# First expert layer of a pooled-attention chain: its last 768 tokens computed as one pair with seven half-depth products

## The chip, the core and the metric

The kernel runs on one core of a Trainium2 chip. The metric is the device time of one execution in microseconds (us); of several runs the median is given. TensorE does the matrix products, VectorE (DVE) and ScalarE (ACT) do the elementwise work and empty the accumulators, GpSimd (POOL) helps them, and SyncE (SP) issues most transfers. Each engine runs its instructions in the order of the program; they meet through semaphores.

## What is computed

Attention over keys and values averaged in groups of 8 (4 batches, 8 heads, 576 positions, 64 channels), then two expert layers over the 2304 tokens of 512 channels:

```python
def _moe_ref(x, w_gate, w_val, w_out):            # 512 -> 1536 -> 512
    gate = 1.0 / (1.0 + np.exp(-(x @ w_gate)))
    val = x @ w_val
    return (gate * val @ w_out).astype(np.float32)

def _moe2_ref(x, w_in, w_out):                    # 512 -> 2048 -> 512
    h = x @ w_in
    sp = np.where(h > 20.0, h, np.log1p(np.exp(np.minimum(h, 20.0))))
    g = h * np.tanh(sp)
    return (g @ w_out).astype(np.float32)
```

All inputs come as 64-bit numbers and are made 32-bit in the kernel; products are made from a high and a low part of each operand (three matmuls: high by high, high by low, low by high).

## The kernel before

**Tiles.** Tokens stand in 18 tiles of 128. The first layer goes through five blocks of 512, 384, 384, 512 and 512 tokens (`sizes`, L67). In a block the 12 slices f of 128 hidden channels follow one another. For each f, `part` (L545) makes the gate `pg` and then the value `pv`, each by 12 matmuls as wide as the block (4 slices of depth, 3 matmuls each); ScalarE makes the sigmoid (L860), VectorE the product (L866), ScalarE its high part (L869) and VectorE its low part (L873, in block 0 a word `G` at L711); `emit_out` (L727) then adds the slice f-1 into four accumulators with 12 more matmuls (`mm3`, L101). `finish` (L733) copies the accumulators out and stores them to `x2d` in DRAM.

**Between the matmuls.** After each of the three groups of 12 matmuls there is a slot (L818). In block 0 the slots run words of a hand-made plan, `START` (L20); the part of it ahead of the first bar runs before block 0. A word is a letter with its numbers and, after a colon, an engine: `m`, `M`, `X`, `N`, `t`, `c`, `p`, `h`, `l` are the attention steps of a tile (scores, maximum, exponent, norm, transpose, copy, values, high and low part of x); `C`, `A`, `B` turn a raw 64-bit weight into its 32-bit parts (scale, bits, high and low part); `K`, `Z`, `V` pool keys and values; `L`, `U`, `J`, `Q`, `R` load. In blocks 1 to 3 the attention of the next block is spread evenly over the slots (`att_tasks`, `batch_tasks`). The second layer's 32 weight pieces are converted in blocks 2 to 4 (`w2_step`): 16 input pieces are stored to `w2d`, 16 output pieces stay in SBUF, in the buffers of first-layer weights that are no longer read. In block 4 the slots prepare the second layer's first operands (`prep_x2`, `prep_w`).

**Second layer.** Three pairs of 2 x 384 tokens. The tokens of a pair and two slices of the weights form a 2 x 2 product that is made by seven half-depth products of sums (`product`, L971, six matmuls of 384 columns each), and `out_unit` (L941) multiplies by the output weights, 512 wide (L933).

**Memory that matters here.** Accumulators: 8 banks, four named `acc0` to `acc3`, two `mm`, two `at`. Output weights of the first layer are stored to `wod` once and read again for each block into a ring of three tiles named `wo` (`load_wo`, L556).

## Time and profile before

| | us |
|---|---|
| median of 3 runs (896.75 to 898.51) | 897.32 |
| span of the profiled execution | 895.9 |
| TensorE busy in it | 885.8 |
| VectorE busy | 520.7 |
| ScalarE busy | 428.3 |
| GpSimd busy | 81.3 |

The span runs from the first to the last instruction of one profiled execution; the median of the timed runs lies 1.4 us above it, for what lies around the instructions. Matmuls overlap: a row that says 0.33 us for one matmul does not say that the next one starts 0.33 us later, and the distance between two starts is what a matmul costs in a row of many.

### The profile page before, as it was taken

The numbers are of one execution on the slowest core, as the hardware profiler recorded it, in microseconds if no ns is written. First come the engines' busy times: TensorE is split into PE (matmuls) and PEld (weight loads), VectorE is DVE, ScalarE is ACT, GpSimd is POOL, SyncE is SP. The second block draws the span as 40 slices with busy tenths as digits, with TensorE's granted clock in tenths as the row PEclk, the third lists the DMA queues.
The fourth block names the chain that finished last, engine by engine and source line by source line (L and its number), as shares of the span: only waits on it lengthen the run. The fifth ranks groups of instructions, "written<-read, shape, count | busy, mean of one in ns | idle before, by whom it ended". The sixth has DMA issues, their size and how long they took to land.

```text
span 895.9 us, 12736 instructions
## 1 busy us (share of the span) xinstructions
PE 885.8 (99%) x4780; PEld 790.3 (88%) x4780; DVE 520.7 (58%) x990; ACT 428.3 (48%) x991; POOL 81.3 (9%) x90
## 2 busy tenths in 40 slices
PE   8999999999999999999999999999999999999998
PEld 7877889999999988888888899998899998999986
DVE  6779864332453332332577467776677767677632
ACT  7756664243454554343445244445454445444431
POOL 3566430100020000000000000000000000000000
PEclk9999999999999999999999999999999999999999
DMA  7788654433575544334665231211121202110001
GB/s 270 227 293 269 223 188 152 135 126 101 166 249 183 172 153 153 118 105 154 211 223 189 71 118 48 83 47 61 35 83 48 83 24 94 59 48 24 1 36 36
DMA packets 42362, 113.33 MB, mean 127 GB/s; under 512 B 5820, under 2 KB 10684, under 8 KB 42300
## 3 DMA queue, kind: packets, MB, share of 16 engines
q1 hardware_dynamic: 41004, 110.25, 37.0%
q10 hardware_dynamic: 1296, 2.26, 0.7%
q8 instruction: 38, 0.62, 0.3%
q14 instruction: 24, 0.20, 0.1%
HBM read 92.42 MB, written 20.07 MB: 126 GB/s over the span
## 4 chain that ended last, share of the span: by engine, by line
PE 90%; DMA 4%; ACT 3%; DVE 2%; issue 1%; SPq 0%; POOL 0%; ACTq 0%; DVEq 0%
PE acc L933 22%; PE p L104 7%; PE p L102 7%; PE p L103 7%; PE acc L102 5%; PE acc L104 5%; PE acc L103 5%; PE pv L550 5%; PE pv L551 5%; PE pv L554 5%; PE pg L550 5%; PE pg L551 5%; PE pg L554 5%; DMA raw<-wv 2%; PE pv L462 2%; PE sc L406 2%
## 5 line engine op out<-in xcount | busy, mean ns | idle before, releaser
L933 PE MATMUL acc<-w,g 128*128 128x512 f32 x864 | 201.3, 390 | 0.0
L933 PEld LDWEIGHTS acc<-w,g 128*128 128x128 f32 x864 | 161.7, 188 | 33.0 <-DVE g L927 0.3
L866 DVE TENSOR_TENSOR sg<-sg,pv 128x512 f32<-128x512 f32 (+1 forms) x58 | 36.5, 629 | 139.5 <-PE pv L554 127.1
L102 PE MATMUL acc<-gh,wo 128*128 128x512 f32 (+1 forms) x240 | 90.2, 376 | 0.0
L103 PE MATMUL acc<-gl,wo 128*128 128x512 f32 (+1 forms) x240 | 88.6, 369 | 0.7 <-DVE gl L711 0.7
L104 PE MATMUL acc<-gh,wo 128*128 128x512 f32 (+1 forms) x240 | 88.4, 368 | 0.0
L550 PE MATMUL pg<-xh,wg 128*128 128x512 f32 (+1 forms) x232 | 86.5, 373 | 0.0
L550 PE MATMUL pv<-xh,wv 128*128 128x512 f32 (+1 forms) x232 | 85.7, 369 | 0.5 <-DVE sg L866 0.5
L551 PE MATMUL pg<-xl,wg 128*128 128x512 f32 (+1 forms) x232 | 85.2, 367 | 0.0
L551 PE MATMUL pv<-xl,wv 128*128 128x512 f32 (+1 forms) x232 | 85.0, 367 | 0.0
L860 ACT ACTIVATE sg<-pg 128x512 f32<-128x512 f32 (+1 forms) x58 | 32.1, 554 | 105.1 <-PE pg L554 104.9
L869 ACT CAST gh<-sg 128x512 fp32r<-128x512 f32 (+1 forms) x60 | 34.9, 582 | 93.7 <-DVE sg L866 93.7
L102 PE MATMUL p<-top,w2s 128*128 128x384 f32 x216 | 72.5, 335 | 0.0
L104 PE MATMUL p<-top,w2s 128*128 128x384 f32 x216 | 72.4, 335 | 0.0
L103 PE MATMUL p<-top,w2s 128*128 128x384 f32 x216 | 72.2, 334 | 0.0
L236 DVE SCALAR_TENSOR_TENSOR cv<-raw,cv 128x512 uint32<-128x512 uint32 x68 | 56.2, 826 | 2.3
L554 PE MATMUL pv<-xh,wv 128*128 128x512 f32 (+1 forms) x232 | 56.9, 366 | 0.0
L554 PE MATMUL pg<-xh,wg 128*128 128x512 f32 (+1 forms) x232 | 56.9, 366 | 0.0
L222 ACT ACTIVATE cv<-raw 128x512 f32<-128x512 f32 x66 | 44.9, 680 | 24.1 <-DMA raw<-wo 10.4
L873 DVE TENSOR_TENSOR gl<-sg,gh 128x384 fp32r<-128x384 f32 (+1 forms) x48 | 30.0, 625 | 36.4 <-ACT gh L869 36.4
L103 PEld LDWEIGHTS acc<-gl,wo 128*128 128x128 f32 x240 | 45.1, 188 | 6.7 <-DVE gl L711 1.0
L102 PEld LDWEIGHTS acc<-gh,wo 128*128 128x128 f32 x240 | 45.1, 188 | 6.7 <-issue 1.3
(150 smaller groups left out, 1674.8 us busy)
## 6 DMA issues: line engine op xcount, KB each, us to landing
wo<-wod SPq DMA_DIRECT2D x48, 512.0 KB
ws<-w2d SPq DMA_DIRECT2D x24, 512.0 KB
raw<-w2i SPq DMA_DIRECT2D x16, 512.0 KB
raw<-w2o SPq DMA_DIRECT2D x16, 512.0 KB
raw<-wv SPq DMA_DIRECT2D x12, 512.0 KB
raw<-wo SPq DMA_DIRECT2D x12, 512.0 KB
wod<-wo SPq DMA_DIRECT2D x12, 512.0 KB
raw<-wg SPq DMA_DIRECT2D x11, 512.0 KB
```

The lines of the kernel that those rows point to most:

```text
L102: nc.tensor.matmul(ps, wt[:, 0, cols], xh, start=start, stop=False)
L103: nc.tensor.matmul(ps, wt[:, 0, cols], xl, start=False, stop=False)
L104: nc.tensor.matmul(ps, wt[:, 1, cols], xh, start=False, stop=stop)
L222: eng.activation(out=f32(c), in_=hi, func=AF.Prelu, scale=BIAS, alpha=-(2.0**32))
L236: nc.vector.scalar_tensor_tensor(out=c, in0=lo, scalar=29, in1=c, op0=ALU.logical_shift_right, op1=ALU.bitwise_or)
L550: nc.tensor.matmul(ps[:, c0:c1], w, xh[:, k, c0:c1], start=(k == 0), stop=False)
L551: nc.tensor.matmul(ps[:, c0:c1], w, xl[:, k, c0:c1], start=False, stop=False)
L554: nc.tensor.matmul(ps[:, c0:c1], w, xh[:, k, c0:c1], start=False, stop=(k == KD - 1))
L860: nc.scalar.activation(out=sg, in_=pg[:, :n], func=AF.Sigmoid)
L866: nc.vector.tensor_mul(out=sg, in0=sg, in1=pv[:, :n])
L869: nc.scalar.copy(out=gh, in_=sg)
L933: nc.tensor.matmul(acc[t][0], g[:, a, c], w[:, b, :], start=(f == 0 and first), stop=(f == NF2 - 1 and last),)
```

## The change

The first layer now goes through three blocks of 512 tokens and then takes the last 768 tokens as one pair of 2 x 384. The pair uses the scheme of the second layer with gate and value in the place of two weight slices: for each f seven products of six matmuls, 384 wide, give gate and value of both halves of the tokens. The sums of weights that this needs (`split_sums`, words `S` and `D`) are made in blocks 1 and 2, stored to `wsd` in DRAM (`z`) and read back in the pair (`load_sums`, `prep_sums`). The sums of tokens are made by words `x` in the last seven slots of block 2, and by `late_rows` after them. The output product of the first half follows one f behind; the gated values of the second half (`g1`) stay in SBUF, and their output product, 12 x 12 matmuls, comes after the last f. GpSimd multiplies gate and value of the second half.

All slots of blocks 0 to 2 now follow the plan, which is new from the start on: attention of tiles 4 to 7 in block 0, 8 to 11 in block 1, 12 to 17 in block 2. Tile 7 is finished inside block 1: for its first f the gate and value are made for 384 tokens, then the words `t7` to `l7` run, then the last 128 tokens follow. All 32 weight pieces of the second layer are converted in blocks 1 and 2 (`d` load, `r` scale, `s` bits, `b` store); the output pieces go to a new DRAM tensor `w2od` and are read back and split in the pair (`split_w2o`). Seventeen of the stores `b` and `z` are issued by ScalarE's queue (`b:a`, `z:a`). In the new part ahead of the first bar and in block 0, eleven conversions have their low part on VectorE (`B:d`; three before) and eight on GpSimd behind ScalarE (`B:a`; nineteen before). The second layer's first operands are prepared during the 12 output steps at the end (`todo`). Work and code of the second layer stay, but its banks start with the accumulators `acc0` to `acc3`.

```diff
--- before.py
+++ after.py
...
+    NG = 384
+    sizes = [NB, NB, NB, 2 * NG]
...
+    w2od = [dram.tile([128, 512], F32, name=f"w2od{i}") for i in range(NF2)]
+    wsd = [dram.tile([128, 2, 512], F32, name=f"wsd{i}") for i in range(NF)]
...
+                if j == NBLK - 1:
+                    c, t0 = divmod(t0, NG)
+                    nc.scalar.copy(out=xs_t[0][:, :, c, t0 : t0 + 128], in_=ps.rearrange("p (k t) -> p k t", k=KD))
+                    return lambda: None
...
+            def split_sums(f):
+
+                t = wpool.tile([128, 2, 512], F32, tag="wo", name="ss", bufs=NWO)
+                G = nc.vector
+                a, b = slice(0, 256), slice(256, 512)
+                for i, nm in enumerate("gv"):
+                    w = w_in_t[nm, f]
+                    settle(w)
+                    G.tensor_add(out=t[:, i, :], in0=f32(w[:, 0, :]), in1=f32(w[:, 1, :]))
+
+                def rest():
+                    G.tensor_sub(out=t[:, 1, a], in0=t[:, 0, a], in1=t[:, 1, a])
+                    G.tensor_sub(out=t[:, 1, b], in0=t[:, 1, b], in1=t[:, 1, a])
+                    G.tensor_add(out=t[:, 0, a], in0=t[:, 0, a], in1=t[:, 1, b])
+                    G.tensor_sub(out=t[:, 0, b], in0=t[:, 0, b], in1=t[:, 1, b])
+
+                rest_of[f] = rest
+                store_of[f] = lambda eng: eng.dma_start(out=wsd[f], in_=t)
...
-                    soon.append(lambda m=m, x=x: nc.sync.dma_start(out=x2d[m][:, o : o + n], in_=x))
+                    later.append(lambda m=m, x=x: nc.sync.dma_start(out=x2d[m][:, o : o + n], in_=x))
...
+                steps = [hi(1, b11), lo(1, b11), sub(b11, b12, b11), hi(5, b11), sub(b12, b22, b12), hi(7, b12), lo(5, b11)]
+                steps += [sub(b11, b22, b11), hi(6, b11), lo(7, b12), lo(6, b11), sub(b12, b21, b11), hi(2, b21), lo(2, b21)]
+                return steps, [hi(4, b12), hi(3, b22), lo(4, b12), lo(3, b22)]
...
+            def load_sums(f):
+                t = sums_of[f] = pa.tile([128, 2, 512], F32, tag="raw", name="sl", bufs=3)
+                nc.sync.dma_start(out=t, in_=wsd[f])
...
+            def prep_sums(f):
+
+                t = sums_of.pop(f)
+                if f % 2:
+                    st = [x1c[:, 1024 * i : 1024 * i + 1024].rearrange("p (a n) -> p a n", a=2) for i in range(2)]
                 else:
+                    st = [px.tile([128, 2, 512], F32R, tag="s", name="s", bufs=2) for _ in range(2)]
+                sum_sets[f] = st
+                for i in (1, 0):
+                    nc.scalar.copy(out=st[i][:, 0, :], in_=t[:, i, :])
+                    nc.vector.tensor_sub(out=st[i][:, 1, :], in0=t[:, i, :], in1=f32(st[i][:, 0, :]))
...
+                    for word in plan[3 * NF * j + k + (1 if j == 0 else 2)]:
+                        run(word)
...
+                    if (j, f) == (1, 0):
+                        c0 = n - 128
+                        pv = ps_mm.tile([128, 512], F32, tag="mm", name="pv")
+                        part(pg, w_in_t["g", f], x_t[1], 0, c0)
+                        part(pv, w_in_t["v", f], x_t[1], 0, c0)
+                        for word in plan[3 * NF + 1]:
+                            run(word)
...
+            late_rows = pr["rows"][1][0][12:] + pr["rows"][0][1] + pr["rows"][1][1]
+            for fn in late_rows:
+                fn()
...
+            banks1 = [(ps_mm, "mm"), (ps_mm, "mm"), (ps_at, "at"), (ps_at, "at")]
+            o3 = blocks[-1][0]
+            wo_c = {}
+            V, A = nc.vector, nc.scalar
+            for f in range(NF):
+                gt, vt = w_in_t["g", f], w_in_t["v", f]
+                sA, sB = sum_sets[f][1], sum_sets[f][0]
+                where = {1: (gt, 0), 2: (gt, 256), 3: (sB, 256), 4: (vt, 256), 5: (sB, 0), 6: (sA, 256), 7: (sA, 0)}
+                a = pg_pool.tile([128, NG], F32, tag="sg", name="a", bufs=2)
+                u, v = (pg_pool.tile([128, NG], F32, tag="gh", name=t, bufs=2) for t in "uv")
+                y = pg_pool.tile([128, NG], F32, tag="gl", name="y", bufs=2)
+
+                def product(k):
+
+                    pool, tag = banks1[k % 4]
+                    ps = pool.tile([128, 512], F32, tag=tag, name=f"q{k}")
+                    wt, c0 = where[k]
+                    for kk in range(2):
+                        xh, xl = pr[k, kk]
+                        mm3(ps[:, :NG], wt, slice(c0 + 128 * kk, c0 + 128 * kk + 128), xh, xl, kk == 0, kk == 1)
+                    return ps[:, :NG]
+
+                wo_c[f] = load_wo(f)
+                p1 = product(1)
+                A.copy(out=a, in_=p1)
+                p6 = product(6)
+                V.tensor_add(out=u, in0=a, in1=p6)
+                p5 = product(5)
+                V.tensor_add(out=v, in0=u, in1=p5)
+                p7 = product(7)
+                V.tensor_add(out=y, in0=v, in1=p7)
+                V.tensor_add(out=u, in0=u, in1=p7)
+                if f + 1 < NF:
+                    prep_sums(f + 1)
+                if f + 2 < NF:
+                    load_sums(f + 2)
+                if f == 0:
+                    emit_out(prev[0], prev[1], prev[2], prev[3], acc_of[prev[0]], prev[4])
+                    finish(prev[0], acc_of.pop(prev[0]), prev[4])
+                    flush()
+                    flush()
+                else:
+                    if f == 1:
+                        acc = acc_tiles()
+                    out_384(wo_c.pop(f - 1), pend, acc, f == 1, False)
+                if f == NF - 1:
+                    wo_c2 = {i: load_wo(i) for i in range(2)}
+                    split_g1(0)
+                    split_g1(1)
+                p2 = product(2)
+                V.tensor_add(out=a, in0=a, in1=p2)
+                A.activation(out=a, in_=a, func=AF.Sigmoid)
+                p4 = product(4)
+                V.tensor_add(out=u, in0=u, in1=p4)
+                V.tensor_mul(out=a, in0=a, in1=u)
+                g = x1c[:, 2048 + 768 * (f % 2) : 2816 + 768 * (f % 2)].rearrange("p (a n) -> p a n", a=2)
+                A.copy(out=g[:, 0, :], in_=a)
+                p3 = product(3)
+                V.tensor_add(out=g1[f], in0=v, in1=p3)
+                A.activation(out=g1[f], in_=g1[f], func=AF.Sigmoid)
+                V.tensor_sub(out=g[:, 1, :], in0=a, in1=f32(g[:, 0, :]))
+                pend = g
+                nc.gpsimd.tensor_mul(out=g1[f], in0=g1[f], in1=y)
+                if f >= 3:
+                    for i in range(2):
+                        if 2 * (f - 3) + i < NF2:
+                            load_w2o(2 * (f - 3) + i)
+                if f >= 4:
+                    for i in range(2):
+                        split_w2o(2 * (f - 4) + i)
+                if f == NF - 1:
+                    load_x2(0, 0)
...
+            for f in range(2):
+                out_384(wo_c2.pop(f), gs.pop(f), acc2, f == 0, False)
+                split_g1(f + 2)
+                wo_c2[f + 2] = load_wo(f + 2)
+            out_384(wo_c.pop(NF - 1), pend, acc, False, True)
+            evict_384(acc, o3)
+            rows0 = prep_x2(0)
+            for _ in range(2):
+                w_sets.append(
+                    [wpool.tile([128, 2, 512], F32R, tag="w", name="w2s", bufs=2 * NF) for _ in range(4)]
+                )
+            todo = {2: rows0[:2], 3: rows0[2:4], 4: rows0[4:]}
+            wrows = [prep_w(ws_of[n_], w_sets[n_]) for n_ in range(2)]
+            todo.update({5: wrows[0][:2], 6: wrows[0][2:], 10: wrows[1][:2], 11: wrows[1][2:]})
+            for f in range(2, NF):
+                out_384(wo_c2.pop(f), gs.pop(f), acc2, False, f == NF - 1)
+                split_g1(f + 2)
+                if f + 2 < NF:
+                    wo_c2[f + 2] = load_wo(f + 2)
+                if f == 5:
+                    load_x2(0, 1)
+                    rows1 = prep_x2(1)
+                    todo.update({7: rows1[:2], 8: rows1[2:4], 9: rows1[4:]})
+                run_all(todo.pop(f))
+            evict_384(acc2, o3 + NG)
```

The slots of block 1's start, of a busy stretch of it and of block 2's end, from the new plan (37 is the part inside block 1's first f):

```text
... m7.0 l6.1 l6.0 B:a M7.0 m7.1 M7.1 G:v X7.0 X7.1 N7:v L2.1 U2.1 Q8 Q9 |
t7.0 t7.1 c7.1:a c7.0:v p7.0 h7.0 p7.1 h7.1 l7.0 l7.1 | d | | K2.0:v m8.0 m8.1 M8.0 L2.2 | ...
M9.1 D1 M9.0 X9.1 r:a b X9.0 V2.2:v s U2.3 U2.5 b:a Q11 V2.5:v d r:a N9:v | ...
x1.9 x0.10 S11 | | x0.11 b x0.12 x1.10 D11 z11:a x0.13 x1.11
```

## Rows read from the trace of the kernel before

**Rows 1.** The page, parts 1 and 2: engines over the span; granted clock by slice.
```profile
PE 885.8 (99%) x4780; PEld 790.3 (88%) x4780; DVE 520.7 (58%) x990; ACT 428.3 (48%) x991; POOL 81.3 (9%) x90
...
PEclk9999999999999999999999999999999999999999
```

**Rows 2.** Busy time by stretch: stretch, its length, busy (count) by engine, clock, DMA share, GB/s.
```profile
0.00:50.00 50.00, 45.80 (x345) 40.60 (x346) 35.91 (x68) 34.88 (x115) 25.19 (x30) 1.00 0.76 258
50.00:100.00 50.00, 47.87 (x251) 38.13 (x250) 43.83 (x67) 31.83 (x74) 31.35 (x27) 1.00 0.81 261
```

**Rows 3.** Waits of TensorE: what waited, for what; us in total, times, longest.
```profile
PE tr L452 <- DVE e L443: 1.3, 2, 1.0
PE pv L462 <- DVE xl L478: 0.7, 2, 0.4
...
PE pv L462 <- ACT pt L94: 0.6, 1, 0.6
```

**Rows 4.** The chain in order of time (start, us): second layer, L933 is 512 wide.
```profile
531.46 4.12 PE acc L933 x18
542.88 4.12 PE acc L933 x18
...
607.28 32.85 PE acc L933 x144
```

**Rows 5.** TensorE in order of time (start, length): a block of 384 tokens.
```profile
199.96 0.33 PE L102 MATMUL acc<-gh,wo 128*128 128x384 f32 x1
...
201.87 0.33 PE L554 MATMUL pg<-xh,wg 128*128 128x384 f32 x1
```

**Rows 6.** The same view: halves of 256 tokens.
```profile
32.82 0.28 PE L551 MATMUL pre<-xl,wv 128*128 128x256 f32 x1
...
33.42 0.66 PE L554 MATMUL pre<-xh,wv 128*128 128x256 f32 x4
```

**Rows 7.** Groups by shape: count | busy us, mean ns of one | idle before.
```profile
L983 DVE TENSOR_TENSOR u<-u,p 128x384 f32<-128x384 f32 x48 | 26.3, 548 | 0.0
L179 DVE TENSOR_TENSOR w2s<-ws,w2s 128x512 fp32r<-128x512 f32 x24 | 16.6, 692 | 8.2 <-ACT w2s L175 8.2
L171 DVE TENSOR_TENSOR ws<-ws 128x256 f32<-128x256 f32 x24 | 10.1, 419 | 0.0
L923 ACT CAST g<-g 128x384 fp32r<-128x384 f32 x48 | 24.1, 514 | 31.0 <-PE acc L933 30.9
L711 POOL TENSOR_TENSOR gl<-sg,gh 128x512 fp32r<-128x512 f32 x5 | 7.1, 1428 | 2.4 <-ACT gh L869 2.4
```

**Rows 8.** VectorE in order of time: neighbours with no wait between them.
```profile
533.56 0.55 DVE L983 TENSOR_TENSOR g<-v,p 128x384 f32<-128x384 f32 x1
534.03 0.55 DVE L983 TENSOR_TENSOR u<-u,p 128x384 f32<-128x384 f32 x1
...
535.22 0.69 DVE L165 TENSOR_TENSOR w2s<-ws,w2s 128x512 fp32r<-128x512 f32 x1 [0.30 <-ACT w2s L160]
535.83 0.69 DVE L168 TENSOR_TENSOR w2s<-ws,w2s 128x512 fp32r<-128x512 f32 x1
```

**Rows 9.** VectorE and GpSimd in order of time, block 0.
```profile
84.13 0.42 DVE L231 TENSOR_SCALAR cv<-cv 128x512 uint32<-128x512 uint32 x1
...
89.20 1.52 DVE L231 TENSOR_SCALAR cv<-cv 128x512 uint32<-128x512 uint32 x1
...
88.59 1.84 POOL L255 TENSOR_TENSOR wo<-cv,wo 128x512 fp32r<-128x512 f32 x1 [0.93 <-ACT wo L94]
```

**Rows 10.** Busy time by stretch: block 0, block 1, one step of the second layer.
```profile
42.58:152.70 110.12, 107.98 (x567) 89.48 (x566) 78.14 (x123) 66.12 (x154) 49.51 (x39) 1.00 0.70 235
152.70:245.00 92.30, 91.98 (x580) 90.67 (x579) 34.98 (x77) 35.78 (x93) 6.00 (x12) 1.00 0.39 126
...
531.40:542.82 11.42, 11.42 (x62) 10.68 (x61) 8.39 (x17) 5.73 (x13) 0.00 (x0) 1.00 0.15 47
```

**Rows 11.** All waits from 100 to 520 us: ScalarE behind VectorE.
```profile
ACT gh L869 <- DVE sg L866: 91.2, 48, 5.6
```

325 lines of the change are left out of this document (151 added, 174 removed).

## The prediction

> **What bounds the kernel now.** [...] A busy TensorE may still be waiting inside, so the stretches come next: only the first 100 us have gaps, 4.2 us in the first 50 and 2.1 in the second [rows 2], and from block 1 on it is busy nearly all the time, 91.98 of 92.30 us [rows 10]. Third, the distance between starts of neighbours, which shows whether busy means full. A step of the second layer is 11.42 us from L933 to L933; 4.12 of it are 18 matmuls of 512 columns, the other 7.30 are 42 of 384, so 0.174 us each [rows 4]. Eleven starts in a 384 block take 1.91 us, again 0.174 [rows 5]. The 512 ones take 32.85 / 144 = 0.228 [rows 4], the 256 ones 0.60 / 5 = 0.120 [rows 6]. These three lie on a line of 0.054 us per 128 columns, with a rest of some 0.012 per matmul. So time is the number of matmuls at their width, and other engines matter only where they make TensorE wait. Its longest wait for VectorE or ScalarE is 1.0 us [rows 3].
>
> **What the pair removes.** Before, 768 tokens take 36 x 2 = 72 matmuls of 384 columns for each f, had they been in two 384 blocks, as two of the five blocks are; the other three stay 512. After, an f of the pair takes 7 x 6 = 42 for gate and value and 24 for the output: 66. Saved: 12 x 6 = 72 matmuls x 0.174 = **-12.5 us**. Attention, second layer and warm-up matmuls keep their counts.
>
> **The split first f of block 1.** 24 matmuls of 512 become 24 of 384 and 24 of 128. On the line above, a 128 one is 0.066, so 24 x (0.174 + 0.066 - 0.228) = **+0.3 us**; bounds 0 (a narrow one as cheap as its columns) and 1.6 (as dear as the 256 row). [...]
>
> **Tile 7 inside that f.** After 24 matmuls of 384 (4.2 us), `t7` to `l7` follow on TensorE with nothing between: `t7` needs the norm of the words just before, `p7` the copies `c7`, and the last 128 tokens need `h7` and `l7`. Those are the waits that the trace has as single events: 0.3 to 1.0 us for the norm, 0.3 to 0.4 for the low part, 0.6 for the copy [rows 3]. Three of them at some 0.5: **+1.5 us**; bounds 0.5 (norm and low part covered) and 3 (each 1.0). Behind them on TensorE the whole of block 1 is late by as much, and nothing gives it back.
>
> **Blocks 0 to 2.** Here I counted the words of the plan and asked what load VectorE gets. In block 0 it was busy 78.1 of 110.1 us, and TensorE lost 2.1 [rows 10]. The new plan moves 13 operations of 0.69 us [rows 7] to it from GpSimd (eight `B:d`, two `B:e` settled later, three `G:v`), 9 us, and one more tile's maxima, norm and copies, some 5: 92 of 110. Against that stand collisions: beside a GpSimd operation of 1.84 us a VectorE shift takes 1.52 us, alone 0.42 [rows 9]; fewer GpSimd operations give back part of these 14 us. In block 1 it was busy 35.0 of 92.3, and TensorE lost 0.3 [rows 10]. Now come 17 bit words (0.42 [rows 9] + 0.69 each: 19), eight scalings by VectorE of two operations (1.3 each: 10), six weight sums (two of 0.69 and four of 0.42 [rows 7]: 18), one more tile (4) and wider products (3): 89 of some 114. Block 2 gets 84 of some 120 in the same way. So three blocks stand at 0.84, 0.78 and 0.70 where the old ones stood at 0.71, 0.38 and less. If each lost what block 0 lost at 0.71, that is 3 x 2.1 - 2.4 = 3.9 more; if the slots cover it as blocks 1 on do now, none. The nearest row by load is block 0's, but the tolerance is long: a value bank is wanted again only 24 matmuls later, a low part 36. I take **+1.5 us** with the new start in it, bounds -2 (the losses of block 0 and part of the start go) and +6 (all three lose as block 0, and the denser block 0 as much again).
>
> [...]
>
> **Entry into the pair.** From the last value of block 2, TensorE has 24 matmuls of 512 and 24 of 384 ahead of it (9.6 us) before `p2` wants the bank of `p6`. VectorE must by then do the last product and low part with ScalarE's cast between (2.0), four `x` operations, five late low parts and four bank reads (13 x 0.47 [rows 8] = 6.1) and `D11` (4 x 0.42 = 1.7): 9.8. Even: **+0.5 us**, bounds 0 and 2 (the sums `S11`, 1.4, late as well).
>
> **Inside the pair** nothing. A step is 54 x 0.174 = 9.4 us; VectorE has nine operations of 384 and four of 512, at the distances of rows 8 (0.47 and 0.61) 6.7 us, a share of 0.71. The second layer lives with 8.39 of 11.42, 0.73, and TensorE loses nothing [rows 10]. If that cover were gone, each 1 us per step would cost 11. GpSimd's product is 384 wide, by its row of 1.43 for 512 [rows 7] about 1.1: it fits as well.
>
> **Exit.** Twelve output steps (144 matmuls) now follow. After the first accumulators are done, VectorE has 34 operations of 384 (four copies, 22 for two sets of tokens, 8 low parts of `g1`): 16.0; and 16 for two weight sets, six of 512 and ten of 256: 7.9; with 0.30 here and there behind ScalarE [rows 8], about 25 us. TensorE has 120 + 24 matmuls of 384, 25.1 us, until `p2` of the second layer wants a bank of the second accumulators, whose copies are last in VectorE's queue. Again even: **+1 us**, bounds 0 and 4 (0.30 on each of 14 high and low pairs). ScalarE, 0.51 per cast [rows 7], has less.
>
> **The sum.** -12.5 + 0.3 + 1.5 + 1.5 + 0.5 + 1.0 = -7.7. On the profiled span 895.9 - 7.7 = 888.2; the median of the runs lies 1.4 above the span, so 889.6.
>
> **Rivals.**
> A. The whole gain arrives: the plan covers all, and the start and block 0 lose less. -12.5 + 0.3 + 0.5 and up to -2: 883.5 to 886.5. For it: old blocks 1 to 4 lose almost nothing. Against: three places have no cover by count.
> B. The end becomes VectorE's: exit and entry at their upper bounds, 4 + 2 in place of 1.5, and tile 7 near 2: about 894.5 (893.5 to 895.5). For it: both sums come out even. Against: durations at full length were used in part.
> C. The saving of matmuls comes, but VectorE bounds blocks 0 to 2 and gives it all back: +6 there with B's 6 and 3 for tile 7: 897.3 - 12.5 + 0.3 + 15 = 900 at most, 897 in the middle (895.5 to 899.1). Then the change doesn't do what it says.
> D. Slower. Seventeen stores stand in ScalarE's queue, and each waits there for VectorE's bits or sums; behind it stand the next sigmoid and cast, and behind those VectorE's product, the bank and TensorE. It decides from 7.7 / 17 = 0.45 us of TensorE per store. At 1.0, the longest such wait [rows 3], it costs 17 in place of the 1.5: 889.6 + 17 - 1.5 = 905. For it: VectorE is at 0.7 to 0.84. Against: ScalarE already waits 91 us for VectorE, up to 5.6 at once, and TensorE doesn't feel it [rows 11].
>
> **Chances.** Forecast 889.6 (its own range 886.5 to 893.5): 0.55. A 0.12, B 0.13, C 0.08, D 0.12. About 0.2%, 1.8 us, is what a measurement of this kernel can tell from no change. Faster is forecast, A and B: 0.80; same is C: 0.08; slower is D: 0.12. The range takes forecast, most of A and B, and ends at 884.0 and 896.0.
>
> **What the new profile would show.** Right: 48 matmuls fewer (-72 + 24) and starts 0.174 apart all through the pair; gaps of TensorE at `t7`, `p7` and the narrow pieces of 1 to 2 us; `p2` of the pair and `p2` of the second layer late by about 1; VectorE near 590 us in all. Wrong: waits of TensorE inside the pair; waits behind casts with a store ahead in ScalarE's queue (D); an exit where TensorE waits for VectorE over several steps (B); a first 100 us with over 8 us of gaps.

## The result, and the profile after

The changed kernel takes **909.79 us** (median of 4 runs, 908.23 to 911.06) against 897.04 before in the same session: a ratio of 1.0136 (95% interval 1.0119 to 1.0152). A second set of runs gave 908.24, 1.0125 (1.0106 to 1.0144). The forecast was 889.6; the time lies above the upper end of its range.

The page of the changed kernel, parts 1 and 2, answers to [rows 1]:

```profile
PE 885.5 (98%) x4732; PEld 783.9 (86%) x4732; DVE 638.7 (70%) x1220; ACT 442.3 (49%) x1021; POOL 79.1 (9%) x91
...
PEclk9999999999999999999999999999999999999999
```

TensorE has 48 matmuls fewer, as forecast, and is yet busy as long as before: a matmul that is slow counts as busy, by its clock (4.75 of 4.80 us at a granted clock of 0.50 in e12, below) as by its operand (11.51 of 11.51 us in a step of the second layer that took 11.42 before), so part of the loss lies inside the busy time and part in waiting. VectorE is busy 638.7 us, 118 more than before. The slices of the clock hide short stretches; the next view has them. It is the busy time by stretch (stretch, length, busy time and count by engine, granted clock, DMA share, GB/s), to be held against [rows 2, 10]: the first two, then blocks 1 and 2, the pair, its exit (the twelve output steps behind it), and one step of the second layer.

```profile
0.00:50.00 50.00, 44.85 (x334) 39.64 (x335) 38.42 (x74) 31.08 (x107) 20.72 (x27) 0.97 0.70 237
50.00:100.00 50.00, 46.52 (x241) 37.45 (x240) 42.52 (x73) 30.71 (x65) 13.03 (x11) 0.97 0.82 272
156.60:268.10 111.50, 111.50 (x570) 92.34 (x569) 80.49 (x158) 45.54 (x117) 9.04 (x14) 1.00 0.74 247
268.10:389.90 121.80, 116.42 (x641) 94.83 (x639) 81.39 (x156) 71.67 (x184) 13.12 (x19) 1.00 0.62 209
389.90:503.80 113.90, 113.70 (x649) 113.05 (x648) 87.07 (x153) 45.42 (x93) 12.21 (x12) 1.00 0.47 170
503.80:529.10 25.30, 22.07 (x121) 20.75 (x121) 21.32 (x44) 13.44 (x30) 0.00 (x0) 1.00 0.73 245
...
540.89:552.40 11.51, 11.51 (x62) 10.77 (x61) 8.49 (x17) 5.47 (x11) 0.00 (x0) 1.00 0.16 48
```

Four things stand out. Block 2 is idle for 5.4 us, the exit for 3.2. The clock is 0.97 in the first two stretches. In block 1 the DMA engines stand at 0.74, where block 1 before had 0.39. And a step of the second layer, which the change does not touch, takes 11.51 us instead of 11.42 while TensorE is busy throughout.

TensorE's waits (what waited, for what: us in total, times, longest), to be held against [rows 3]:

```profile
PE pv L532 <- DVE sg L866: 2.8, 1, 2.8
PE ac L122 <- DMA wo<-wod: 2.1, 2, 1.6
PE sc L408 <- ACT xs L491: 1.4, 1, 1.4
PE tr L454 <- DVE e L445: 1.4, 1, 1.4
...
PE sc L408 <- DMA q<-qt: 1.0, 1, 1.0
```

No name carries the loss. It is spread over many tiles, which is what a delay further up looks like. The waits of the other engines between 160 and 395 us show where it starts; before, no such wait for raw weights stood in these blocks:

```profile
ACT cv L244 <- DMA raw<-w2o: 12.1, 4, 5.0
DVE cv L246 <- DMA raw<-w2o: 5.0, 1, 5.0
ACT cv L244 <- DMA raw<-w2i: 4.8, 2, 4.5
```

ScalarE and VectorE stand still for 22 us behind loads of raw weights, with everything that is queued behind these words. One of them in order of time (start, length, engine, instruction, idle time before it and its releaser):

```profile
252.58 0.88 SPq L232 DMA_DIRECT2D raw<-w2o  x1
259.03 0.33 SPq L540 DMA_DIRECT2D wo<-wod  x1
...
260.23 0.38 SPq L232 DMA_DIRECT2D raw<-w2o  x1
...
267.99 0.66 ACT L244 ACTIVATE cv<-raw 128x512 f32<-128x512 f32 x1 [5.03 <-DMA raw<-w2o]
268.56 0.60 ACT L869 CAST gh<-sg 128x512 fp32r<-128x512 f32 x1
...
269.19 1.15 DVE L873 TENSOR_TENSOR gl<-sg,gh 128x512 fp32r<-128x512 f32 x1 [3.41 <-ACT gh L869]
...
275.08 1.04 PE L454 MATMUL tr<-ident,e 128*72 128x128 f32 x8 [1.39 <-DVE e L445]
```

For five and a half microseconds SyncE issues nothing, with the output weights `wo` at the head of its queue. What they wait for is a place in their ring, which TensorE is still reading (waits of SyncE, 250 to 262 us):

```profile
SPq L540 <- PE acc L124: 5.5, 1, 5.5
```

The kernel before has such waits too, 56.5 us in 12 between 146 and 520 us, but there no raw load came late by them. Here the raw load behind goes out at 260.23 and is there at 267.99. ScalarE has waited 5.03 us for it, then makes the cast that VectorE has waited 3.41 us for, the exponents and maxima of the next tile follow late, and 7 us further on TensorE waits for the norm.

**Where the 12 us are.** For each stretch I take its length and subtract its matmuls at the distances they have where nothing waits (0.2272 us for 512 columns, 0.1735 for 384, 0.120 for 256, 0.111 for 128). By these distances the matmuls take 11.1 us less than before. What is left over is the gaps of TensorE, in us (the rows named e, f and h are experiments, told below):

| kernel | start | block 0, tile 7 | block 1 | block 2 | pair | exit | second layer | all |
|---|---|---|---|---|---|---|---|---|
| before | 9.9 | 5.2 | 3.2 for blocks 1 to 4 | | | | 1.3 | 19.6 |
| changed | 12.5 | 9.2 | 1.5 | 9.5 | 1.4 | 4.5 | 3.2 | 41.9 |
| changed, again | 12.4 | 7.0 | 1.5 | 9.0 | 1.4 | 5.4 | 3.2 | 39.8 |
| e1_shared_raw | 14.3 | 8.6 | 1.5 | **4.9** | 1.4 | 5.8 | 3.2 | 39.7 |
| e3_old_front | **9.5** | **6.8** | 1.5 | 11.2 | 1.4 | 6.1 | 3.2 | 39.7 |
| e4_gap | 9.9 | 11.6 | 1.5 | 6.8 | **0.9** | 5.1 | **1.1** | 37.0 |
| e6_exit | 10.6 | 6.5 | 1.5 | 9.2 | 1.4 | **3.7** | **6.1** | 39.0 |
| e9_loads_earlier | 10.5 | 6.5 | **7.9** | **12.5** | 1.4 | 4.3 | 3.2 | 46.4 |
| f1_scalings_later | 10.4 | 6.9 | 1.5 | **9.3** | 1.4 | 5.9 | 3.2 | 38.6 |
| h1_exit_lead | 13.1 | 7.3 | 2.5 | 8.1 | 1.4 | **2.5** | 3.2 | 38.1 |
| h2_front_gap_later_lead | 9.8 | 7.7 | 1.5 | 9.9 | 0.9 | 2.6 | 1.4 | 33.7 |

Bold is what the edit was aimed at. Gaps grew by 22.3, matmuls shrank by 11.1: 11.2 us longer, and the span grew by 11.4 (895.9 to 907.3). The columns that an edit does not touch say how far one execution differs from the next: with the new plan, start and block 0 together have 16.7 to 22.8 in fourteen profiles, and block 2, where nothing was aimed at it, 6.8 to 9.6, or 11 to 15 with a stretch at half clock in it. So a single profile settles no question of a few us by a total, and the timed runs of the changed kernel spread over 3 to 6 us where those of before spread over 2 to 4. The first 100 us have 8.6 us without work, which the prediction had named as a sign that it is wrong.

### The profile page after: what moved, and what is told of

Its sections match the earlier page's. It is cut to its first block, busy times and chain, and to the rows that moved or that the text cites. A ratio compares the mean times of both kernels' runs of the same rounds, so it can differ in the third digit from the quotient of the medians.

```text
span 907.3 us, 13087 instructions
## 1 busy us (share of the span) xinstructions
PE 885.5 (98%) x4732; PEld 783.9 (86%) x4732; DVE 638.7 (70%) x1220; ACT 442.3 (49%) x1021; POOL 79.1 (9%) x91
## 4 chain that ended last, share of the span: by engine, by line
PE 80%; DMA 7%; DVE 6%; ACT 4%; issue 2%; POOL 1%; SPq 0%; ACTq 0%; POOLq 0%; DVEq 0%
PE acc L1075 22%; PE p L122 7%; PE p L124 7%; PE p L123 7%; PE acc L122 3%; PE acc L124 3%; PE acc L123 3%; PE q L122 3%; PE q L123 3%; PE q L124 3%; PE pv L532 3%; PE pv L533 3%; PE pv L536 2%; PE pg L532 2%; PE pg L533 2%; PE pg L536 2%
## 5 line engine op out<-in xcount | busy, mean ns | idle before, releaser
L122 PE MATMUL acc<-gh,wo 128*128 128x512 f32 x144 | 58.1, 403 | 0.0
L124 PE MATMUL acc<-gh,wo 128*128 128x512 f32 x144 | 56.3, 391 | 0.0
L123 PE MATMUL acc<-gl,wo 128*128 128x512 f32 x144 | 56.2, 390 | 0.0
L866 DVE TENSOR_TENSOR sg<-sg,pv 128x512 f32<-128x512 f32 x34 | 23.3, 685 | 37.7 <-PE pv L536 34.5
L869 ACT CAST gh<-sg 128x512 fp32r<-128x512 f32 x36 | 22.3, 621 | 55.5 <-DVE sg L866 55.4
L1069 DVE TENSOR_TENSOR g<-g,g 128x384 fp32r<-128x384 f32 x48 | 26.6, 557 | 32.2 <-ACT g L1065 31.8
L431 ACT ACTIVATE e<-sc,mx 128x72 f32<-128x72 f32 x140 | 42.8, 327 | 5.0 <-DVE mx L419 4.7
L860 ACT ACTIVATE sg<-pg 128x512 f32<-128x512 f32 x34 | 20.3, 598 | 46.2 <-PE pg L536 46.0
L123 PEld LDWEIGHTS p<-top,w2s 128*128 128x128 f32 x216 | 40.6, 188 | 1.0
L122 PEld LDWEIGHTS p<-top,w2s 128*128 128x128 f32 x216 | 40.5, 188 | 1.0
L124 PEld LDWEIGHTS p<-top,w2s 128*128 128x128 f32 x216 | 40.6, 188 | 0.0
L123 PE MATMUL p<-x1c,w2s 128*128 128x384 f32 x120 | 40.5, 337 | 0.0
L1132 ACT ACTIVATE g<-g 128x384 f32<-128x384 f32 x24 | 12.6, 527 | 57.1 <-DVE g L1125 57.1
L122 PE MATMUL p<-x1c,w2s 128*128 128x384 f32 x120 | 40.4, 337 | 0.0
L124 PE MATMUL p<-x1c,w2s 128*128 128x384 f32 x120 | 40.2, 335 | 0.0
```

The lines of the kernel that those rows point to most:

```text
L122: nc.tensor.matmul(ps, wt[:, 0, cols], xh, start=start, stop=False)
L123: nc.tensor.matmul(ps, wt[:, 0, cols], xl, start=False, stop=False)
L124: nc.tensor.matmul(ps, wt[:, 1, cols], xh, start=False, stop=stop)
L431: nc.scalar.activation(out=e_t[T][:, 4 * g + h, :], in_=s[:, h, :], func=AF.Exp, scale=-1.0, bias=mx_t[T][:, 4 * g + h, :], accum_out=sm_t ...
L866: nc.vector.tensor_mul(out=sg, in0=sg, in1=pv[:, :n])
L1069: nc.vector.tensor_sub(out=g[:, 1, :], in0=src, in1=f32(g[:, 0, :]))
```

## The experiments

Times are medians with the ratio to the kernel before of the same session (897.0 to 898.3) and its interval.

### Blocks 1 and 2: who is late?

Theory: the loads of raw weights. Rivals: the stores in ScalarE's queue (rival D of the prediction), VectorE's load.

**e1_shared_raw** loads every fourth raw piece only.

```diff
+                if share and len(shared) % 4:
+                    shared.append(shared[-1])
+                    raw_q.append(shared[-1])
+                    return
```

> Only every fourth word d of blocks 1 and 2 loads a raw weight piece; the three after it are converted from the same raw tile (so three quarters of the second layer's weights are left out). All work of ScalarE, VectorE and TensorE and all stores stay. Theory L (late loads): in the changed kernel ScalarE and VectorE stand 22 us in blocks 1 and 2 for raw pieces that land 7 to 8 us after their issue, and the attention steps queued behind them make TensorE wait; without them TensorE's gaps in block 2 fall from 9.5 us to about 3 and the time from 909.8 to about 903. Rival V (VectorE's load of about 0.75 in these blocks is the cause): gaps and time stay within 1 us. Rival S (stores in ScalarE's queue): the same, within 1 us.

903.17 us, 1.0069 (1.0039 to 1.0098). Of the waits for raw weights from 160 to 395 us one line is left:

```profile
DVE cv L254 <- DMA raw<-w2o: 5.0, 1, 5.0
```

TensorE's waits of 1.4, 1.4 and 1.2 us in block 2 of the changed kernel are gone with them; the longest that is left is

```profile
PE tr L462 <- POOL e L453: 0.8, 1, 0.8
```

Block 2's gaps are 4.9, below those of every other profile (6.8 at the least, 9.0 and 9.5 in the changed kernel's two). Theory kept: 2 to 5 us of the loss come with these loads. The 4.9 that stay, where blocks 1 to 4 before had 3.2 together, no run here explains.

**e2_stores_sp** gives the seventeen stores back to SyncE's queue (`b:a` becomes `b`, `z2:a` becomes `z2`, and so on).

> The 17 stores z and b that ScalarE's queue issues go to SyncE's queue; nothing else changes. Rival S (the slow case D of the prediction, a store holds ScalarE until VectorE is done): 3 to 8 us less, 902 to 907. Theory L: the loads land no sooner and SyncE gets 17 more waits ahead of its loads, so between no change and 3 us more, 909 to 913. Rival V: no change.

905.45, 1.0093 (1.0065 to 1.0120). The waits for raw weights stay (22 us by its trace), block 2 keeps 9.6 us of gaps, block 1 has 2.8 instead of 1.5. So the stores are not what blocks 1 and 2 lose by. The median, though, lies in the range that rival S gave, and the profile is of the slowest of the four executions (908.57; two others took 903.6 and 903.7), so where those gained it doesn't show. That the stores cost something elsewhere stays open.

**e5_no_rest_of_sums** leaves out the words `D`, 48 operations of VectorE.

```diff
-                        rest_of.pop(a[0])()
+                        rest_of.pop(a[0])
```

> The words D do nothing: four of the six VectorE operations of each weight sum are left out (12 x 1.5 us of VectorE in blocks 1 and 2; the stored sums are not the right ones). Rival V (VectorE's load makes TensorE wait): block 2's gaps fall by 3 us or more, the time by as much against the changed kernel in this group. Theory L (late loads): gaps of block 2 within the 6.8 to 9.6 us that the same words have had so far, the time within 1.5 us.

907.47, 1.0126 (1.0092 to 1.0160). VectorE is busy 20 us less in all, and block 2's gaps are 9.7, some 8 without the stretch at half clock that this profile has there. They did not fall below what the same words show elsewhere, so VectorE's load is not what block 2 pays for.

**e8_even_words** spreads the words `d`, `r`, `s`, `b` evenly over the slots of blocks 1 and 2, with four slots between a load and its scaling.

> Only the places of the words d, r, s, b in blocks 1 and 2 change: a raw piece is scaled 4 slots (block 1) or 3 slots (block 2) after its load in place of 1 to 5, all by ScalarE, its bits follow a slot later, all stores go by SyncE; and the first sum is read back six slots later so that it does not hold one of three raw buffers. No work is left out. Theory L: the waits for raw pieces in these blocks go from 22 us to under 5, block 2's gaps to about 4, the time falls by 4 to 6 us. Rival V: the same operations on VectorE but for ten scalings (13 us less), so under 2 us. Rival Q (the attention chains and their two banks make the waits in any order of the other words): gaps in block 2 stay at 7 to 9.

917.19, 1.0227 (1.0214 to 1.0240): a miss. The waits for raw weights are gone (0.5 us), but TensorE now waits 4.6 us for `q`, 4.4 for `e` and 2.6 for `vb`; gaps of 6.3 in block 1 and 15.1 in block 2.

**e9_loads_earlier** moves nine loads and three scalings only.

```diff
-V2.6:p r:v O8 d r:a S2 D2 | z2:a O9 s o8 | |
+V2.6:p r:v O8 d S2 D2 | r:a z2:a O9 s o8 | |
...
-                    if last and k == SL - 8:
+                    if last and k == SL - 2:
```

> The changed kernel with nine of its loads of the second layer's raw weights issued one to three slots earlier, three of the scalings that wait for them one or two slots later, and the first weight sum read back from DRAM at SL-2 instead of SL-8, so that it does not share the DMA engines with the raw weights of block 2. Nothing is left out; no instruction is added. Theory (late loads): ScalarE and VectorE wait 22 us for raw weights between 156 and 390 us in the changed kernel; with the loads about 4 to 7 us earlier this falls to about 8, the gaps of TensorE in block 2 fall from 9 to about 5, and the time falls by about 4 us, to about 905. Rival (the work of block 2 itself is too much for the engines beside TensorE, the waits for loads only take its place): the waits fall as well, block 2 keeps its 9 us of gaps, and the time stays within 1 us of 909.

913.53, 1.0188 (1.0166 to 1.0210): slower than the changed kernel, against both expectations. TensorE's waits tell why:

```profile
PE sc L375 <- DMA q<-qt: 4.3, 3, 3.3
PE pv L431 <- POOL vb L346: 4.3, 1, 4.3
```

The raw loads now stand ahead of loads of keys, values and `q` in SyncE's queue, and wait there for a free raw buffer, 19.0 us in 7 waits between 156 and 395 us. One late load has been traded for another that TensorE needs sooner.

**f1_scalings_later** leaves every load where it is and moves seven scalings by one or two slots.

> The changed kernel with seven of the second layer's scalings (those that waited 1.8 to 5.0 us for their raw weights) put one or two slots later in the plan, and the loads left where they are, so that SyncE's queue is the same. Nothing is left out. Theory (late loads cost because ScalarE and VectorE stand still in order behind them): the waits for raw weights between 156 and 390 us fall from 22 us to under 8, no load of q or v becomes late, block 2's gaps of TensorE fall from 9 to about 5 and the time by about 4 us. Rival (the loads are late as a whole, and each step that is moved later makes the loads behind it late in its turn, since a raw buffer comes free later): the waits move to other loads, block 2 keeps 9 us, and the time stays within 1.5 us.

906.12, 1.0098 (1.0078 to 1.0117). Waits from 263 to 385 us:

```profile
DVE cv L220 <- ACT cv L211: 8.5, 3, 5.1
...
ACT cv L211 <- DMA raw<-w2o: 4.2, 1, 4.2
```

The waits for the loads have fallen to 4.2 us, and VectorE now waits 8.5 us for the scalings. Block 2 keeps 9.3 us of gaps: the rival. The median is 2 to 4 us lower than the changed kernel's; its profile has no stretch at half clock. Taken together: with the loads gone a good part of block 2's loss goes, with the loads present moving the words only chooses who waits. Whether the DMA engines' share (0.62 to 0.74) or SyncE's one queue is what makes them late was not separated.

### Start and block 0

**e3_old_front** takes the plan before for the start and block 0, with the steps of tile 7 put into it.

> The old words ahead of block 0 and in its slots, with tile 7's words m to N, and the loads L2.0 L2.1 U2.1 Q9 that the new ones have there, put into the last slot of block 0. Theory L with the start: the 2.96 us gap at 55.8 us goes, which came behind a late raw piece, and so does the half clock after it; gaps up to the end of block 0 fall by 5 to 7 us, the time to about 904. Rival T7 (one more tile in front of block 1 costs what is lost there, in whatever order): gaps up to 156 us stay within 2 us of the changed kernel's 21.7, time 908 to 911.

906.55, 1.0099 (1.0084 to 1.0114). Start and block 0 together have 16.3 us of gaps, where the changed kernel's two profiles have 21.7 and 19.4. But the four profiles with the old front have 16.3, 16.4, 17.5 and 19.5, the fourteen with the new one 16.7 to 22.8: medians 17.0 and 19.1, the ranges overlap. So the new plan costs some 2 us here, less than the single edit seemed to say; what makes it more in one execution are single pauses and the clock behind them, as here in the changed kernel (TensorE, then ScalarE, in order of time):

```profile
55.08 1.07 PE L536 MATMUL pg<-xh,wg 128*128 128x512 f32 x4
58.94 0.50 PE L532 MATMUL pv<-xh,wv 128*128 128x512 f32 x1 [2.80 <-DVE sg L866]
59.28 0.40 PE L533 MATMUL pv<-xl,wv 128*128 128x512 f32 x1
...
60.20 0.63 PE L532 MATMUL pv<-xh,wv 128*128 128x512 f32 x1
60.63 0.63 PE L533 MATMUL pv<-xl,wv 128*128 128x512 f32 x1
...
55.78 0.66 ACT L244 ACTIVATE cv<-raw 128x512 f32<-128x512 f32 x1 [2.41 <-DMA raw<-wv]
```

A late raw load holds ScalarE, TensorE pauses 2.8 us, and soon after it starts again its matmuls come 0.43 us apart instead of 0.23.

### The clock behind a pause

**e12_probe_one_gap** puts one pause into the kernel before.

```diff
+                    if (j, f) == (4, 4):
+                        probe = ps_at.tile([128, 512], F32, tag="at", name="probe")
+                        z = px.tile([128, 128], F32, name="z")
+                        for _ in range(6):
+                            nc.gpsimd.tensor_add(out=z, in0=sg[:, 0:128], in1=sg[:, 128:256])
+                        nc.tensor.matmul(probe[:, :128], z, ident, start=True, stop=True)
```

> The kernel before with one probe in block 4 at f=4, behind the products on v: six additions of 128x128 on GpSimd in a row and one matmul of 128 columns that waits for the last of them. The probe's result is used by nothing; all other work stands. It makes one pause of TensorE of about 3 to 4 us where the kernel before has none. Theory (a pause of 3 us is followed by a stretch at half the granted clock): the profile shows the granted clock at half for about 3.4 us behind the pause, which costs about 1.7 us more, so the time is 4.5 to 6 us above the kernel before. Rival (the half-clock stretches of the changed kernel come from elsewhere): the clock stays full and the time rises by the length of the pause alone, 3 to 4 us.

907.41, 1.0107 (1.0092 to 1.0121): 9.9 us for one pause. Busy time by stretch, before, in and behind the pause, and TensorE in order of time:

```profile
449.00:458.00 9.00, 9.00 (x41) 7.46 (x40) 7.13 (x14) 4.75 (x10) 0.00 (x0) 1.00 0.53 180
458.00:464.70 6.70, 0.47 (x3) 0.05 (x1) 5.63 (x9) 1.88 (x4) 3.77 (x6) 0.85 0.59 218
464.70:469.50 4.80, 4.75 (x12) 3.89 (x13) 0.00 (x0) 0.00 (x0) 0.00 (x0) 0.50 0.55 188
469.50:474.00 4.50, 4.50 (x21) 3.70 (x21) 0.00 (x0) 1.06 (x3) 0.00 (x0) 1.00 0.00 0
...
464.75 0.80 PE L872 MATMUL probe<-ident,z 128*128 128x128 f32 x2 [6.28 <-POOL z L871]
...
466.19 0.63 PE L104 MATMUL acc<-gh,wo 128*128 128x512 f32 x1
466.62 0.63 PE L102 MATMUL acc<-gh,wo 128*128 128x512 f32 x1
```

The pause came out at 6.3 us, longer than meant. The granted clock falls to 0.50 inside it and stays there for 4.8 us of work, in which matmuls of 512 start 0.43 us apart: 2.4 us on top. The rest is a wait of 2.4 us at a transpose in block 0 (in the kernel before 1.0), which the probe does not touch. So the rival is out: a pause alone, put into the old kernel, brings the half clock. It does not always. In the twenty profiles here TensorE made 31 pauses of over 2 us after the first 9 (distance of two starts less the matmul's own); 18 were followed by a stretch at half clock, the eight longest among them, and 13 were not, two of over 3 us included. Eight more such stretches stand behind no single pause of over 2 us. The kernel before has neither.

### The address of the moving operand

**e4_gap** puts the spare tile back that the change had dropped; nothing reads it, but it moves the tiles behind it.

```diff
+                        gap = px.tile([128, 88], F32, name="gap")
+                        nc.gpsimd.memset(gap[:, 0:1], 0.0)
```

> The pool on the right side gets back the spare tile of 88 numbers that the change dropped, so the 18 tiles named top lie 352 bytes lower; nothing else changes. Theory P (place): matmuls that read top start 0.176 us apart in the changed kernel and 0.173 before, at other addresses; they come back to 0.173, some 860 of them, and the time falls by about 2 us to 907.5. Rival B (the order of the banks or the second layer's other tiles): the distance stays 0.176 and the time 909.8.

904.08, 1.0083 (1.0056 to 1.0110). The chain through the second layer, first the changed kernel, then this one (start, length; one line each step):

```profile
540.89 4.12 PE acc L1075 x18
...
552.40 4.12 PE acc L1075 x18
```

```profile
549.29 4.12 PE acc L1077 x18
...
560.72 4.12 PE acc L1077 x18
```

A step takes 11.51 us without the spare tile and 11.43 with it, as before [rows 4]. In the second layer, matmuls that read `top` start 0.1760 us apart without, 0.1730 with it (medians over the trace). The gaps of the second layer go from 3.2 to 1.1 and those of the pair from 1.4 to 0.9: 2.6 us in all, near the 2 that theory P gave. The median lies lower still, by 4 to 6 us; what is above 2.6 of that this edit does not account for. Why that address is slower these runs do not say.

### The exit

**e6_exit** loads the first of the second layer's weight sets later and prepares one of its first two weight sets a step later.

> In the 12 output steps at the end, the first weight set of the second layer is loaded three steps later, so that it does not compete with the output weights of the third step, and the second set is prepared in the second layer's first step instead. Theory X (the exit loses 4.5 to 6.1 us by a late output weight, 1.7, and by VectorE and ScalarE that lag behind, the rest): gaps there fall to 2 or less and the time by 3 to 4 us. Rival: the loss only moves into the second layer's first step, whose gaps rise by as much, and the time stays within 1.

908.89, 1.0137 (1.0123 to 1.0152). The exit's gaps fall to 3.7, the second layer's grow from 3.2 to 6.1: the work is late there instead, as the rival had it.

**e10_exit_loads** issues the two loads of scaled weights after f=2 and f=6 and gives ScalarE all the evictions.

> The changed kernel with the two scaled-weight loads of the second layer's first step issued after f=2 and f=6 of the output steps instead of ahead of them, and all evictions of the running sums at the exit of the pair given to ScalarE. Nothing is left out. Theory (the exit is bound by the output weights' loads, which share the DMA engines with those two 1 MB loads, and then by VectorE, which shares the evictions with its splits): the gaps between the end of the pair and the second layer fall from 4.5 to 5.4 us to about 2.5, the second layer's own 3.2 stay, and the time falls by 2 to 3 us. Rival (the sum of VectorE's work from the exit to the second layer's second step is the bound, wherever it waits): what the exit gains comes back in the second layer's first steps, as 5 to 6 us there, and the time stays within 1 us.

909.25, 1.0125 (1.0107 to 1.0143), a miss for the theory as for the rival (the loads that the theory calls 1 MB are 512 KB each): the second layer keeps 3.2, the exit has 6.9 us of gaps (half clock of 3.4 us among them). The first wait for output weights is gone; waits of 2.0 for ScalarE's casts and 2.1 for later output weights stand in its place.

**f2_exit_half_loads** loads every second of the later tiles of output weights.

```diff
-                    wo_c2[f + 2] = load_wo(f + 2)
+                    wo_c2[f + 2] = wo_c2[f + 1] if f % 2 else load_wo(f + 2)
```

> The changed kernel with five of the ten loads of output weights from the third f of the exit on left out (an odd f uses the tile of the f before), which leaves out part of the output weights' product. It takes 2.5 MB from the DMA engines in the 25 us of the exit, and no work from any other engine. Theory (DMA engines bind the exit): TensorE's gaps there fall from 4.5 to under 2.5. Rival (VectorE and ScalarE bind it: splits of the gates, of the second layer's rows and weights, evictions): they stay within 0.7 us of what they were behind the first wait, which this kernel leaves (1.7 us at 503.6). The time falls by 2 us by the theory and by less than 1 us by the rival.

909.18, 1.0117 (1.0081 to 1.0153). The first wait stays, 1.6 us, though the trace now puts it to a split by ScalarE (`top`) and not to a load; behind it the gaps are 1.8 instead of 2.8. That is between theory and rival, and the time, with 12.2 us of gaps in block 2, says nothing about it.

**f3_exit_low_gpsimd** lets GpSimd make the low parts of the gates.

```diff
-                    V.tensor_sub(out=t[:, 1, :], in0=g1[f], in1=f32(t[:, 0, :]))
+                    nc.gpsimd.tensor_sub(out=t[:, 1, :], in0=g1[f], in1=f32(t[:, 0, :]))
```

> The changed kernel with the low parts of the gates' split at the exit (twelve subtractions of 128x384) made by GpSimd instead of VectorE. Nothing is left out. Theory (VectorE binds the exit, which is busy 24 of 26 us there): its busy time falls by about 12 x 0.42 = 5 us, TensorE's gaps fall from 4.5 to about 3, the time by 1.5 us. Rival (GpSimd's operations slow VectorE's beside them, as the shift that took 1.52 instead of 0.42 us did): VectorE's busy time stays or grows, each subtraction on GpSimd takes 1 us or more and its consumer waits, gaps 5 to 7 us, the time 1 to 3 us longer.

910.18, 1.0137 (1.0120 to 1.0155); gaps of 6.4. Busy time from 504 to 530 us, the changed kernel first:

```profile
504.00:530.00 26.00, 22.85 (x126) 21.65 (x127) 22.17 (x46) 13.75 (x30) 0.00 (x0) 1.00 0.71 236
```

```profile
504.00:530.00 26.00, 23.43 (x130) 22.00 (x129) 22.36 (x38) 13.97 (x29) 8.41 (x7) 1.00 0.64 202
...
PE ac L122 <- DMA wo<-wod: 5.0, 3, 2.4
```

VectorE, busy 22.2 us here before the edit and not the 24 of the expectation, has 8 operations fewer and is busy as long: 22.36 / 38 = 0.59 us each instead of 22.17 / 46 = 0.48. That is what the rival had, so the run does not tell what a less busy VectorE would give. What TensorE waits for in it is output weights, 5.0 us, and nothing else.

**h1_exit_lead** gives those loads two more places and starts each one earlier, with no work taken away; the scaled weights come after them.

```diff
-                t = ws_of[n_] = pa.tile([128, 2, 512], F32, tag=f"x{'hl'[n_]}0", name="ws", bufs=1)
-                nc.sync.dma_start(out=t, in_=w2d[n_])
+                t = wo_c2[n_ + 2] = pa.tile([128, 2, 512], F32R, tag=f"x{'hl'[n_]}0", name="wo", bufs=1)
+                nc.sync.dma_start(out=f32(t), in_=wod[n_ + 2])
...
-                wo_c2[f + 2] = load_wo(f + 2)
+                wo_c2[f + 4] = load_wo(f + 4)
```

> The changed kernel with two more places for output weights at the exit: the third and fourth tile of them are loaded into the two places that are free when the pair ends (where the change loads the second layer's scaled weights), each later one starts one f earlier, and the scaled weights come after them, at f=2 and f=3. Nothing is left out and no work is added. Theory (the loads of output weights start too late for their landing time): TensorE's waits for them at the exit, 2 to 5 us in the runs so far, fall below 0.5, the gaps of the exit from 4.5 to about 2, and the time by 2 to 3 us. Rival (VectorE and ScalarE bind the exit): the waits for output weights vanish as well, waits for ScalarE's and VectorE's tiles take their place, gaps 4 us or more, and the time stays within 1 us.

905.61, 1.0077 (1.0048 to 1.0105). TensorE's waits between 495 and 530 us:

```profile
PE ac L122 <- DMA wo<-wod: 1.2, 1, 1.2
PE ac L122 <- ACT x1c L155: 0.8, 1, 0.8
```

The exit's gaps fall to 2.5, below every other profile (h2, with the same exit, has 2.6), and nothing comes back behind it. About half of the exit's loss was the landing of output weights (512 KB for every 12 x 0.1735 = 2.08 us of matmuls, next to other loads). Of the rest, these two waits are the named part: once more a load, and a split by ScalarE. The times say less than the profile: they run from 900.5 to 917.5.

### Together

**best_all** has the old front with tile 7, the spare tile, the moves of e9 and the exit of e10.

> All corrections in one: the plan of the kernel before for blocks 0 and 1 with only the tile 7 steps of the change put into it, the earlier loads of the raw weights, the spare tile that puts the moving operand back at its old address, and the loads at the exit as in the kernel that changes the exit alone. Nothing is left out. If the losses named are separate and add (start and block 0 about 4 to 5, late loads 4, the address 2.5, exit 2 to 3), the time is about 909 - 13.5 = 895.5, range 892 to 899: level with the kernel before or just under it. If they stand in for each other (one queue is late whatever else is mended), it stays above 902.

908.77, 1.0126 (1.0103 to 1.0149), a miss: the moves of e9 cost 8.0 and 11.0 us of gaps in blocks 1 and 2, with stretches at half clock behind pauses of 4.3 and 3.2 us.

**f4_front_and_gap** has only the front and the spare tile.

> The plan before for the start and block 0 with the steps of tile 7 put into it, and the spare tile that puts the moving operand back at its old address; all else is the changed kernel. Nothing is left out. If the two single edits add (start and block 0: gaps of 16 to 17 instead of 18 to 22; the address 2.5), block 1 keeps 1.5, block 2 about 9 and the exit about 4.5: total gaps about 34 instead of 41.9, the time about 901.5, range 899 to 905. Rival (what the front gains, the later loads take back, as in the kernel with all corrections): block 1 or block 2 grows by what the front gives, and the time stays above 905.

903.37, 1.0057 (1.0036 to 1.0078), inside the range that the sum of the two edits gave; block 0 has a stretch of 6.8 us at half clock in the profile.

**h2_front_gap_later_lead** adds the later scalings of f1 and the exit of h1.

> The plan before for the start and block 0 with the steps of tile 7, the spare tile, the seven scalings later, and the exit with more lead. Nothing is left out. From the single edits: the first two together gave 903.4, the scalings later about 3 us less than the changed kernel, the lead 2 to 3 us: 903.4 - 5.5 = about 898, range 895 to 902, within 0.3% of the kernel before. If the waits only change places, it stays at 901 or above.

**898.88 us, 1.0013 (0.9998 to 1.0029)**: level with the kernel before, as the single edits summed. Its profile has no stretch at half clock. 33.7 us of gaps are left against 19.6; 8.2 of the difference are in blocks 1 and 2. No version here beats the kernel before.

## Why the prediction was wrong

**Matmuls, right.** 48 fewer, -12.5 us. TensorE does not wait inside the pair (gaps 1.4 with the entry and the address in it; the forecast had 0.5).

**The split first f, mis-sized.** Its term was 0.3. The 128-wide pieces start 0.111 us apart in the changed kernel's TensorE, the line of [rows 4, 6] had given 0.066. The trace of the kernel before had a row of that width, which the prediction did not use: its warm-up matmuls, six of them in 0.83 us, of which the last takes 0.28, so 0.11 apart. That row first, then two of the pieces:

```profile
10.66 0.83 PE L593 MATMUL warm<-ident 128*128 128x128 f32 x6
...
151.57 0.28 PE L532 MATMUL pg<-x,wg 128*128 128x128 f32 x1
151.68 0.28 PE L533 MATMUL pg<-x,wg 128*128 128x128 f32 x1
```

24 x (0.174 + 0.111 - 0.227) = 1.4, inside the bounds.

**Tile 7, right:** 1.1 us (0.51, 0.25 and 0.35) for 1.5.

**Blocks 0 to 2, the step that failed.** The term was 1.5 with a bound of 6; measured are 13.4 in the profile shown: 5.6 in start and block 0, two stretches at half clock of some 1.7 each among them, and 7.8 in blocks 1 and 2. (In the second profile of the same kernel they are 10.5.) The step counted VectorE's work, and asked nothing of the loads. The count itself came out near, even high: VectorE is busy 85.2, 80.5 and 81.4 us in the three blocks where the step had 92, 89 and 84. (The 590 for the whole kernel, 638.7 measured, doesn't follow from the prediction's own counts, and old block 2 stood at 0.43, not at 0.38 or less.) What the count left out had a row: block 1 stood at a DMA share of 0.39, block 0 at 0.70 [rows 10], and the plan brought 32 raw loads of 512 KB, their stores and the sums into two blocks, to 0.74 and 0.62. The share alone would not have told where it hurts: block 1 at 0.74 has 1.5 us of gaps, and old block 2 (245 to 335 us) at 0.58 kept TensorE busy throughout. Taking some 20 us of work off VectorE changed nothing in block 2 (e5, gaps of 9.7), taking the loads away did (e1, 4.9): an engine that runs in order stood behind a late load, up to 5.0 us at once, however little else it had to do. Nor did the step price a pause at more than its length. Of the 7.8 in blocks 1 and 2 the runs put 2 to 5 to these loads, of the 5.6 ahead of them some 2 to the new plan and 3.4 in this profile to the half clock; the rest stays open.

**Exit, mis-sized.** The term was 1.0, bounds 0 and 4, measured 4.5 to 5.4. It again counted VectorE against TensorE, 25 us against 25.1; measured are 21.3 us of VectorE in 25.3. Missing was the landing time of the output weights, which are read again here at 512 KB for each f and make about half of the loss (h1). The other half stays open between a further load and ScalarE's splits; no trace of the changed kernel's exit shows TensorE waiting for VectorE there.

**The second layer, not in the sum.** The dropped tile `gap` stood in the diff, and the sum had no term for it; it costs 2.4 to 2.6 us.

**The rivals.** D came nearest (905, slower, 0.12), but by luck as far as blocks 1 and 2 go: without stores in ScalarE's queue block 2 loses as much (e2). B and C had VectorE as the bound; e5 and TensorE's waits at the exit speak against it.

Forecast -7.7. In its place: -12.5 + 1.4 + 1.1 + 13.4 + 4.5 + 2.4 and 0.9 at the entry and the rest of the pair, +11.2 us; the span grew by 11.4.

## What to carry to other kernels

A step that is moved brings its loads along: ask which engine stands in order behind each load, what stands ahead of that load in its queue, and what that waits for. Bytes and the DMA share of a stretch are a first hint, no more: block 1 at a share of 0.74 had 1.5 us of gaps, block 2 at 0.62 had 9.5. A pause of TensorE can cost more than its length (6.3 us and another 2.4 at half clock in e12; the eight longest of the 31 pauses all had such a stretch behind them), so many small losses and one long one need not cost the same. A tile that nobody reads may be there for the address of the next one (matmuls 0.1760 us apart without it, 0.1730 with it, e4): time the change without it before it goes.

## What the runs showed of the hardware

- Behind 18 of 31 pauses of over 2 us the granted clock stood at 0.50 for a stretch, and matmuls of 512 columns started 0.43 us apart instead of 0.23; one such stretch of 4.8 us of work cost 2.4 us (e12). Two executions of the same code differ in this: the changed kernel's two profiles have two such stretches and one, and its times run from 905.75 to 911.97.
- The distance of two matmuls depended on where the moving operand lay: 0.1760 or 0.1730 us at 384 columns, by a spare tile of 88 numbers per partition (e4).
- Matmuls of 128 columns start 0.111 us apart, those of 256 0.120 [rows 6]: between the two, width hardly counts.
- VectorE's operations grew from 0.48 to 0.59 us on average while GpSimd subtracted beside them (f3); why, this run does not say. What it cost TensorE was not separated, since it waited for loads there.
